# Batch 0 of a spectral filter ahead of an MLP: both filter products from one spectrum, the inverse tables built earlier, and matmuls on ones between the stages

## The chip, the cores and the metric

One core of a Trainium2 chip (trn2). The metric is the device time of one execution in microseconds (us), the median over runs. The kernel before takes 773.71 us (9 runs, 773.45 to 774.46).

## What is computed

The reference has two layers that follow each other. The first filters along the sequence in the frequency domain, the second is an MLP with an exact GELU. Cut to what matters:

```python
# x: (8, 3008, 256); filt_r, filt_i: (1505, 256); w_in: (256, 2048); w_out: (2048, 256)
X = np.fft.rfft(x, axis=1)
Y = X * (filt_r + 1j * filt_i)[None, :, :]
y = np.fft.irfft(Y, n=3008, axis=1).reshape(8 * 3008, 256)
h = y @ w_in
out = (0.5 * h * (1.0 + erf(h / np.sqrt(2)))) @ w_out
```

All arrays are float32 in DRAM. On the chip the operands are bf16 and the sums float32.

## The kernel before

**The transform.** 3008 = 47 x 64. A transform of that length is made as matmuls with small tables: a stage over 47 points (table `T1`, stage 1), a twiddle and a stage over 64 points (`T2`, stage 2), the product with the filter, the inverse over 64 points (`T3`, stage 3) and the inverse over 47 points (`T4`, stage 4). With real input 24 values of the first frequency index (`K1 = 24`) are enough, and they are worked on in 12 pairs p. The tables are not loaded: they are computed at the start. DVE makes angles (`table_1`, `table_2_angle`), ACT takes their sine, and the matrix with real and imaginary parts exchanged comes from a matmul with a signed permutation (`table_2_swap`, L194). `T3` is `T2` transposed on PE (`table_3`, L230).

**Batches 1 to 7.** Their four stages (`s1`, `s2`, `s3`, `s4`) are small and are spread between the matmuls of the MLP of the batch before, at slots that are written out by hand (`put`). A slot is one `mm2` step (4 matmuls with `w_out`, L488) and one `mm1` step (2 matmuls with `w_in`, L461, and a GELU on ACT, L464). Between `s1` and `s2`, and between `s3` and `s4`, the data go through DRAM (`R1`, `R2`) to be re-ordered. `r1` and `r2` read them back. For batch 1 the slots are a list of their own: first slots of `s1`, `s2`, `s4`, their spacing, and the slots of `r1` and `r2`.

**Batch 0.** Nothing can hide it: the MLP has no input before it is through. It runs in a form of its own which stays on the chip, with the channels on partitions where the other batches have the sequence:

- `c1` (L361), 16 steps u: stage 1 of a group of 4 columns and one half of the channels. Steps u = 0 to 3 need the first two of eight transfers of x, steps 4 to 7 the next two, and so on. ACT or DVE empties each result into `at_sb`.
- `c1t` (L371), 6 steps: 8 transposes on PE, emptied into `b_sb`.
- `c2` (L383, L388), 12 steps p: stage 2. The product with the filter needs (real, imaginary) times the filter's real part, and (-imaginary, real) times its imaginary part. Before, `T2` holds three columns (-imaginary part, real, imaginary), PE makes both forms of the spectrum with 4 matmuls, and one DVE multiplication over 128 x 1024 (L388) makes both products. The last pair is done in two halves (L392).
- `c3` (L405): stage 3, both products are summed in PSUM against the same `T3`. ACT empties it into `vt_sb`.
- `c3t`, `c4` (L424, L438): transposes and stage 4, into `y_sb`, which `mm1` reads.

The filter arrives in partitions 0 to 63 of `F` (`load_filters`, L91) and is needed in partitions 64 to 127 as well. Before, `dup_filters` (L96) copies it, for the pairs p = 0, 1 on DVE and for the other ten on POOL, one copy for each pair.

**What sets the order.** The program is under a manual schedule: every engine runs its instructions in the order in which the Python code issues them, and an instruction that waits holds up all that stand behind it on its engine. The only choice left is that of PSUM buffers. The order of the prelude is written out in the kernel's main function: table work is put between the steps of `c1` and `c2`. All loads of x, the filter and the MLP weights are issued by POOL, so they stand in one line with POOL's copies. `warm_up(n)` issues n matmuls of 512 columns on a tile of ones, whose results nobody reads.

Of the kernel before, what the change touches and what calls it, by code (L numbers as in the profile page):

```python
# [21 lines left out]
TCH = 512  # L22

# [5 lines left out]
class _Mix:  # L29
    def __init__(self, ctx, tc, x, filt_r, filt_i, w_in, w_out, out):  # L30
# [23 lines left out]
        self.T2 = c.tile([128, K1, 3, NB], BF16, name="T2")  # L54
# [19 lines left out]
    def load_x(self, b, lo=0, hi=4, hs=(0, 1)):  # L74
        nc = self.nc
        if lo == 0 and 0 in hs:
            self.st[b, "x"] = self.px.tile([128 if b else 2 * NA, HB, 256], BF16, tag="x", name="x_sb")
        xt, o = self.st[b, "x"], 64 if b else NA
        xv = self.x[b].rearrange("(n1 h c w) d -> h c n1 w d", h=2, c=4, w=8)
        for c in range(lo, hi):  # L80
            for h in hs:
                nc.gpsimd.dma_start(out=xt[h * o:h * o + NA, c * 8:c * 8 + 8, :], in_=xv[h, c])  # L82
# [14 lines left out]

    def gate(self, t):

        g = self.po.tile([1, 1], BF16, tag="gate", name="gate")  # L100
        self.nc.gpsimd.tensor_copy(out=g, in_=t)  # L101

    def load_next(self, b, p, c, h):

        self.gate(self.st[b, "p", p][0:1, 0:1])
        self.load_x(b + 1, c, c + 1, (h,))
# [17 lines left out]
    def table_1(self, g):  # L124
# [3 lines left out]
        k48 = self.iota(g, "k48", [128, 2, K1], [[0, 2], [1, K1]])  # L128
        off = g.tile([128, 2, K1], FP32, name="off")
        nc.gpsimd.memset(off[:, 0, :], 0.25)  # L130
        nc.gpsimd.memset(off[:, 1, :], 0.5)
# [7 lines left out]
        nc.vector.scalar_tensor_tensor(out=w, in0=k48, scalar=n1, in1=off, op0=ALU.mult, op1=ALU.add)  # L139
# [6 lines left out]
    def table_2(self, g):  # L146
# [8 lines left out]
        self.n2, ri = col("n2"), col("ri")  # L155
        v.tensor_copy(out=self.n2, in_=m_i)
        v.tensor_copy(out=ri, in_=ri_i)
        ts(out=self.n2, in0=self.n2, scalar1=1.0 / self.S, scalar2=None, op0=ALU.mult)
        ts(out=ri, in0=ri, scalar1=-0.25, scalar2=0.25, op0=ALU.mult, op1=ALU.add)
        self.jn = g.tile([128, NB], FP32, name="jn")  # L160
        ts(out=self.jn, in0=self.jj, scalar1=self.n2, scalar2=ri, op0=ALU.mult, op1=ALU.add)
        self.n12, self.sg, self.to = col("n12"), col("sg"), col("to")
        ts(out=self.n12, in0=self.n2, scalar1=float(K1 // 2), scalar2=None, op0=ALU.mult)

        ts(out=self.sg, in0=ri, scalar1=8.0, scalar2=-1.0, op0=ALU.mult, op1=ALU.add)
        v.tensor_tensor(out=self.to, in0=self.p, in1=self.sg, op=ALU.add)

    def unit_matrices(self, g, cols):
        ts = self.nc.vector.tensor_scalar
        self.eye, self.swap = (g.tile([128, 128], BF16, name=n) for n in ("eye", "swap"))  # L170
        ts(out=self.eye, in0=cols, scalar1=self.p, scalar2=None, op0=ALU.is_equal)
        ts(out=self.swap, in0=cols, scalar1=self.to, scalar2=self.sg, op0=ALU.is_equal, op1=ALU.mult)

    def table_2_angle(self, h):

        v, k = self.nc.vector, K1 // 2
        w, r = self.gen[:, h], self.gen[:, 2]
        if h == 0:
            v.scalar_tensor_tensor(out=w, in0=self.kk.unsqueeze(2).to_broadcast([128, k, NB]), scalar=self.n2,
                                   in1=self.jn.unsqueeze(1).to_broadcast([128, k, NB]), op0=ALU.mult, op1=ALU.add)  # L180
        else:
            v.tensor_scalar(out=w, in0=self.gen[:, 0], scalar1=self.n12, scalar2=None, op0=ALU.add)
        v.tensor_scalar(out=r, in0=w, scalar1=RND, scalar2=-RND, op0=ALU.add, op1=ALU.add)
        v.tensor_tensor(out=w, in0=w, in1=r, op=ALU.subtract)

    def table_2_sin(self, h):
        self.nc.scalar.activation(out=self.T2[:, 12 * h:12 * h + 12, 1, :], in_=self.gen[:, h], func=AF.Sin,
                                  scale=2.0 * PI)

    def table_2_swap(self, h):  # L190
        t2 = self.T2[:, 12 * h:12 * h + 12]
        for i in range(2):
            ps = self.bank("ps_sw", "n")
            self.nc.tensor.matmul(ps[:, 0:384], lhsT=self.swap, rhs=t2[:, :, 1, 32 * i:32 * i + 32],  # L194
                                  start=True, stop=True)
            self._evac(t2[:, :, 2, 32 * i:32 * i + 32], ps[:, 0:384].rearrange("p (k j) -> p k j", k=12),
                       "act", 1.0 - 2.0 * i)
            if h == 1:
                self._evac(t2[:, :, 0, 32 * i:32 * i + 32], ps[:, 0:384].rearrange("p (k j) -> p k j", k=12),
                           "act", 2.0 * i - 1.0)  # L200

    def table_2_minus(self):
        t2 = self.T2[:, 0:12]
        self.nc.vector.tensor_scalar(out=t2[:, :, 0, :], in0=t2[:, :, 2, :], scalar1=-1.0, scalar2=None, op0=ALU.mult)

    def weights_4(self, g):

        nc, v = self.nc, self.nc.vector
        ts = v.tensor_scalar
        col = lambda name: g.tile([128, 1], FP32, name=name)  # L210
        q, c = col("q"), col("c48")
        ts(out=c, in0=self.p, scalar1=48.0, scalar2=None, op0=ALU.is_ge)
        v.scalar_tensor_tensor(out=q, in0=c, scalar=-48.0, in1=self.p, op0=ALU.mult, op1=ALU.add)
        self.wt = col("wt")
        ts(out=self.wt, in0=q, scalar1=2.0, scalar2=1.0, op0=ALU.is_ge, op1=ALU.add)
        self.wtc = col("wtc")
# [10 lines left out]
    def table_3(self, q, eng):  # L227
        ps = self.bank("ps_t3", "n", BF16)
        for i in range(8):
            self.nc.tensor.transpose(ps[:, 128 * i:128 * i + 128],  # L230
                                     self.T2[:, 8 * q + i, 1:3].rearrange("p a b -> p (a b)"), self.eye)

        self._evac(self.T3[:, 8 * q:8 * q + 8], ps.rearrange("p (k n r) -> p k r n", k=8, r=2), eng)

    def warm_up(self, n):

        ps = self.bank("ps_warm", "w")
        for i in range(n):
            self.nc.tensor.matmul(ps[:, i % 2], lhsT=self.ones[:, 0:128], rhs=self.ones, start=True, stop=True)
# [50 lines left out]
    def s2(self, b, p):  # L290
        nc = self.nc
        ps = self.bank("ps_s2")
        for i in range(2):
            k = 2 * p + i
            nc.tensor.matmul(ps[:, 256 * i:256 * i + 256], lhsT=self.T2[:, k, 1:3].rearrange("p a b -> p (a b)"),  # L295
# [70 lines left out]
    def c1t(self, q, eng):  # L366
# [6 lines left out]
        self._evac(b[:, 0:4, :].rearrange("p a b -> p (a b)"), ps, eng)  # L373

    def c2(self, p):
# [4 lines left out]
        for t, o in ((0, 1), (1, 0)):  # L380
            for i in range(2):
                k = 2 * p + i
                nc.tensor.matmul(ps[:, t, 256 * i:256 * i + 256],  # L383
                                 lhsT=self.T2[:, k, o:o + 2].rearrange("p a b -> p (a b)"),
                                 rhs=self.st[0, "b", k // 4][:, k % 4, :], start=True, stop=True)
        f = self.F[:, :, 2 * p:2 * p + 2, :]
        if p < 11:
            nc.vector.tensor_tensor(out=w, in0=ps, in1=f.rearrange("p t a b -> p t (a b)"), op=ALU.mult)  # L388
            return
        w, ps = (v.rearrange("p t (a b) -> p t a b", a=2) for v in (w, ps))  # L390
        for c in (slice(0, 128), slice(128, 256)):
            nc.vector.tensor_tensor(out=w[:, :, :, c], in0=ps[:, :, :, c], in1=f[:, :, :, c], op=ALU.mult)  # L392

    def c3(self, p, np=2):

        if p == 0:
            self.vt = self.pg.tile([128, 2, 97, 32], BF16, tag="g", name="vt_sb")
        ps = [self.bank("ps_c3", "n") for half in range(2)]
        for i in range(np):
            w = self.st[0, "p", p + i]  # L400
            for half in range(2):
                for k in range(2):
                    for t in range(2):
                        c, o = 128 * (2 * i + k), 256 * k + 128 * half
                        self.nc.tensor.matmul(ps[half][:, c:c + 128], lhsT=w[:, t, o:o + 128],  # L405
                                              rhs=self.T3[:, 2 * (p + i) + k].rearrange("p a b -> p (a b)"),
                                              start=t == 0, stop=t == 1)
# [5 lines left out]
    def c3t(self, u):  # L413

        if u == 0:

            self.nc.gpsimd.memset(self.vt[:, :, 96, :], 0.0)
# [89 lines left out]
def kernel(  # L507
# [16 lines left out]
    m.psum(wide, w=(2, 2), n=(4, 1))  # L524
    act = "act"
    m.p = m.iota(g, "p", [128, 1], [[0, 1]], cm=1)
    m.load_x(0, 0, 1, (0,))
    m.pi = m.iota(g, "pi", [128, 1], [[0, 1]], cm=1, dt=I32)
    m.load_x(0, 0, 1, (1,))
# [4 lines left out]
    m.weights_4(g)  # L534
# [3 lines left out]
    m.kk = m.iota(g, "kk", [128, K1 // 2], [[1, K1 // 2]])  # L538
    m.jj = g.tile([128, NB], FP32, name="jj")
    for sgn, lo in ((1, 0), (-1, 32)):  # L540
        nc.gpsimd.iota(m.jj[:, lo:lo + 32], pattern=[[sgn * NA, 32]], base=min(0, sgn * NA),
                       channel_multiplier=0, allow_small_or_imprecise_dtypes=True)
    cols = m.iota(g, "cols", [128, 128], [[1, 128]])
    m.load_x(0, 1, 4)
    m.gen = m.py.tile([128, 3, K1 // 2, NB], FP32, tag="y", name="gen")
    m.table_2(g)
    m.table_2_angle(0)
    m.unit_matrices(g, cols)
    m.table_2_angle(1)
    for k, n in ((0, 4), (4, 4), (8, 8), (16, 8)):  # L550
        m.load_filters(k, n)
    m.dup_filters(nc.gpsimd, 4, 4)
    m.load_w_in()
    m.dup_filters(nc.gpsimd, 8, 8)


    warm = g.tile([128, 1], FP32, name="warm")
    for u in range(16):
        m.c1(u // 2, u % 2, act if u < 4 or u % 2 else False)
        if u == 3:  # L560
            m.warm_up(3)
            m.table_2_sin(0)
        if u == 7:
            m.table_2_swap(0)
            m.table_2_minus()
            m.warm_up(3)
            m.table_2_sin(1)
        if u == 11:
            m.warm_up(2)

    nc.scalar.activation(out=warm, in_=m.p, func=AF.Gelu)
# [113 lines left out]
```

## Time and profile before

| | us |
|---|---|
| median of 9 runs | 773.71 |
| the profiled execution, its own time | 773.71 |
| its span in the trace | 771.9 |

The 1.8 us between the last two lie around the span. Cutting the span at the points where the work changes gives, for busy times in us:

| stretch of the span | PE | DVE | ACT | POOL | what runs there |
|---|---|---|---|---|---|
| 0 to 5.8 | 4.34 | 3.33 | 1.84 | 4.77 | `warm_up`, `T1`, first transfers of x |
| 5.8 to 14.0 | 6.83 | 8.05 | 6.63 | 5.68 | `c1`, first half of the tables |
| 14.0 to 31.4 | 16.28 | 15.45 | 16.36 | 17.19 | `c1t`, `c2`, `c3`, `T3`, filter copies |
| 31.4 to 39.9 | 7.11 | 6.73 | 6.03 | 4.11 | `c3t`, `c4` |
| 39.9 to 50.3 | 10.14 | 9.06 | 7.46 | 0.00 | `mm1` of the first tile, `s1` of batch 1 |
| 50.3 to 771.9 | 713.08 | 354.54 | 529.00 | 32.79 | MLP, batches 1 to 7 between |

Busy times count an engine's overlapping instructions once. PE's ends are modelled, so a busy PE is not PE at its peak. The granted TensorE clock is 1.00 in every stretch. In the lists of the trace a row has its start, the time from the first start to the last end of the instructions merged in it, engine, line, operation, tiles and count. What stands in brackets is the engine's idle time before it and what ended it.

### The profile page before, as it was taken

The numbers are of one execution on the slowest core, as the hardware profiler recorded it, in microseconds if no ns is written. First come the engines' busy times: TensorE is split into PE (matmuls) and PEld (weight loads), VectorE is DVE, ScalarE is ACT, GpSimd is POOL, SyncE is SP. The second block draws the span as 40 slices with busy tenths as digits, with TensorE's granted clock in tenths as the row PEclk, the third lists the DMA queues.
The fourth block names the chain that finished last, engine by engine and source line by source line (L and its number), as shares of the span: only waits on it lengthen the run. The fifth ranks groups of instructions, "written<-read, shape, count | busy, mean of one in ns | idle before, by whom it ended". The sixth has DMA issues, their size and how long they took to land.

```text
span 771.9 us, 14958 instructions
## 1 busy us (share of the span) xinstructions
PE 757.8 (98%) x5965; PEld 528.4 (68%) x6066; DVE 397.1 (51%) x722; ACT 567.3 (73%) x981; POOL 64.5 (8%) x160
## 2 busy tenths in 40 slices
PE   8999999999999999999999999999999999999998
PEld 5847675676776766667677767666776776766666
DVE  8856755464555645457463664637646366411011
ACT  6879955897568975699656996579865798666663
POOL 8801100020000200011000110001100000000000
PEclk9999999999999999999999999999999999999999
DMA  9894745466154661636516464354553422410111
GB/s 144 144 192 115 151 114 126 131 126 157 49 140 109 136 161 41 191 77 127 139 53 181 85 133 123 80 153 98 121 137 82 138 83 69 123 42 28 42 42 55
DMA packets 87398, 85.66 MB, mean 111 GB/s; under 512 B 6752, under 2 KB 77536, under 8 KB 87328
## 3 DMA queue, kind: packets, MB, share of 16 engines
q1 hardware_dynamic: 78816, 68.70, 31.1%
q0 software_dynamic: 8512, 16.00, 14.1%
q8 instruction: 47, 0.77, 0.4%
q14 instruction: 23, 0.19, 0.1%
HBM read 54.00 MB, written 46.66 MB: 130 GB/s over the span
## 4 chain that ended last, share of the span: by engine, by line
PE 92%; POOL 3%; DMA 2%; issue 1%; ACT 1%; DVE 0%; POOLq 0%; SPq 0%
PE ps_o L488 43%; PE ps_h L461 39%; PE ps_s L320 3%; PE ps_s L345 3%; PE ps_s L295 2%; PE ps_s L272 2%; DMA x_sb<-in_x_dram 2%; POOL F L96 1%; POOL x_sb L82 1%; POOL F L91 1%; DMA d_sb<-R 0%; PE ps_e L478 0%; ACT g_sb L464 0%; ACT p L301 0%; ACT p L302 0%
## 5 line engine op out<-in xcount | busy, mean ns | idle before, releaser
L464 ACT ACTIVATE g_sb<-ps_h 128x512 bf16<-128x512 f32 x752 | 437.9, 597 | 183.4 <-PE ps_h L461 155.4
L488 PE MATMUL ps_o<-w_out_sb,g_sb 128*128 128x256 bf16 x2992 | 447.8, 273 | 2.0
L461 PE MATMUL ps_h<-y_sb,w_in_sb 128*128 128x512 bf16 (+3 forms) x1500 | 424.8, 366 | 0.8 <-DMA x_sb<-in_x_dram 0.7
L488 PEld LDWEIGHTS <-g_sb 128*128 128x128 bf16 x2992 | 283.6, 98 | 134.5 <-issue 9.9
L461 PEld LDWEIGHTS <-w_in_sb 128*128 128x128 bf16 x1600 | 154.6, 98 | 23.9 <-issue 1.1
L494 DVE COPY ost<-ps_o 128x512 f32<-128x512 f32 x93 | 63.8, 686 | 143.5 <-PE ps_o L488 143.5
L303 DVE TENSOR_TENSOR p<-ps_s,F 128x512 bf16<-128x512 f32 x84 | 58.1, 691 | 105.9 <-ACT p L302 89.4
L249 DVE TENSOR_SCALAR y_sb<-ps_s 128x376 bf16<-128x376 f32 x112 | 60.9, 548 | 80.9 <-PE ps_s L345 80.9
L247 DVE CAST a_sb<-ps_s 128x512 bf16<-128x512 f32 x112 | 69.3, 682 | 27.7 <-PE ps_s L272 27.7
L247 DVE CAST v_sb<-ps_s 128x512 bf16<-128x512 f32 x84 | 57.3, 684 | 3.0 <-PE ps_s L320 3.0
L301 ACT ACTIVATE p<-ps_s 64x512 bf16<-64x512 f32 x84 | 49.8, 593 | 2.0
L302 ACT CAST p<-ps_s 64x512 bf16<-64x512 f32 x84 | 48.5, 577 | 1.0
L345 PEld LDWEIGHTS <-d_sb 96*128 96x128 bf16 x448 | 30.8, 97 | 25.8 <-DMA d_sb<-R 0.7
L101 POOL COPY gate<-p 1x1 bf16<-1x1 bf16 x48 | 8.5, 176 | 470.8 <-DVE p L305 470.8
L345 PE MATMUL ps_s<-T,d_sb 96*128 96x94 bf16 x448 | 36.4, 205 | 1.5 <-DMA d_sb<-R 0.4
L305 DVE TENSOR_TENSOR p<-p 128x512 bf16<-128x512 bf16 x84 | 35.7, 425 | 2.9
L304 DVE TENSOR_TENSOR p<-p,F 128x512 bf16<-128x512 bf16 x84 | 34.8, 415 | 0.0
L320 PE MATMUL ps_s<-p,T 128*128 128x256 bf16 x168 | 32.1, 273 | 2.2 <-DVE p L305 0.2
L82 POOL DMA_DIRECT2D x_sb<-in_x_dram x64 | 32.5, 510 | 13.1 <-issue 12.6
L295 PE MATMUL ps_s<-b_sb,T 128*128 128x256 bf16 x168 | 32.1, 273 | 0.0
L320 PEld LDWEIGHTS <-T 128*128 128x128 bf16 x168 | 16.3, 98 | 20.1 <-DVE p L305 0.5
L295 PEld LDWEIGHTS <-T 128*128 128x128 bf16 x168 | 16.4, 98 | 13.4
(103 smaller groups left out, 189.5 us busy)
## 6 DMA issues: line engine op xcount, KB each, us to landing
out_dram<-ost SPq DMA_DIRECT2D x93, 256.0 KB, 2.4
x_sb<-in_x_dram POOLq DMA_DIRECT2D x64, 188.0 KB, 3.6
R<-a_sb SPq DMA_DIRECT2D x112, 96.0 KB, 2.1
b_sb<-R SPq DMA_DIRECT2D x28, 384.0 KB, 4.1
R<-v_sb SPq DMA_DIRECT2D x42, 256.0 KB, 3.3
d_sb<-R SPq DMA_DIRECT2D x56, 192.0 KB, 4.6
w_in_sb<-in_moe_w_in_dram POOLq DMA_DIRECT2D x2, 512.0 KB, 8.0
w_out_sb<-in_moe_w_out_dram POOLq DMA_DIRECT2D x2, 512.0 KB, 11.5
```

The costliest lines, as they stand in the source:

```text
L247: self.nc.vector.tensor_copy(out=out, in_=in_)
L249: self.nc.vector.tensor_scalar(out=out, in0=in_, scalar1=scale, scalar2=None, op0=ALU.mult)
L295: nc.tensor.matmul(ps[:, 256 * i:256 * i + 256], lhsT=self.T2[:, k, 1:3].rearrange("p a b -> p (a b)"), rhs=self.st[b, "b", k // 6][:, k % ...
L301: nc.scalar.activation(out=p2[0:64], in_=ps[64:128], func=AF.Copy, scale=-1.0)
L302: nc.scalar.copy(out=p2[64:128], in_=ps[0:64])
L303: nc.vector.tensor_tensor(out=p1, in0=ps, in1=f(0), op=ALU.mult)
L320: nc.tensor.matmul(ps[:, 256 * i:256 * i + 256], lhsT=self.T3[:, k].rearrange("p a b -> p (a b)"), rhs=w[:, 256 * i:256 * i + 256], start= ...
L345: nc.tensor.matmul(ps[:, 94 * i:94 * i + 94], lhsT=d[:, (grp % 2) * 4 + i, 128 * half:128 * half + 128], rhs=t4, start=True, stop=True)
L461: nc.tensor.matmul(ps[:, o:o + n], lhsT=self.w_in_sb[:, dc, jc * 128:jc * 128 + 128], rhs=self.ring[:, dc, off:off + n], start=(dc == 0), ...
L464: nc.scalar.activation(out=self.st["g", t][:, jc, :], in_=ps, func=AF.Gelu)
L488: nc.tensor.matmul(ps[:, tile_i % 2, :], lhsT=g[:, jc, tile_i * 128:tile_i * 128 + 128], rhs=self.w_out_sb[:, jc, :], start=(jc == 0), sto ...
L494: nc.vector.tensor_copy(out=ost, in_=ps)
```

## The change

- **One spectrum.** `T2` loses its third column. `c2` makes 2 matmuls into one PSUM bank instead of 4 into two, and the DVE multiplication reads this bank twice (a broadcast operand of the same 128 x 1024 elements). The factor i goes into a second inverse table `T3i`: `c3` multiplies the product with the filter's imaginary part by `T3i`. `T3i` is `T3` with its two columns exchanged and a sign for each partition; it is made by two DVE instructions for k = 0 to 7 and two for 8 to 15 (`table_3_turn`), and by two ACT instructions from PSUM for 16 to 23.
- **Angles by shifts.** The angle in turns is kept between 64 and 128, so that a left shift of its bits by 15 leaves the fraction as a signed 32-bit integer; ACT reads that and scales it by 2 pi / 2^32. This takes the place of two rounding passes per half.
- **Table order.** The first sine stands ahead of `c1` u = 0 on ACT instead of behind u = 3. The swap of the first half, and the transposes of `T3` for k = 0 to 7, stand on PE between `c1` u = 3 and u = 4 (before: the swap behind u = 7, the transposes among the `c2` steps). The second sine and its swap stand between u = 7 and u = 8 (before: the sine there, the swap behind `c2` p = 1). The second third of `T3` stands ahead of `c1t`. `T4c`'s matmul moves from q = 4 to u = 11.
- **Filter.** Three parts of 8 instead of 4, 4, 8, 8. Its second copy is made by DVE for p = 0, 1, by a transfer from SBUF to SBUF on the SP queue for p = 2, 3 and p = 8 to 11, and by POOL for p = 4 to 7.
- **Issue order on POOL.** The first two transfers of x stand ahead of the index tile `p`; `w_in`'s loads move behind the copies, directly ahead of x of batch 1. Some small constants move from DVE to POOL or back.
- **The rest.** 42 matmuls on ones instead of 20. PSUM is cut otherwise (w, m, n = 2, 1, 5 banks; then v, t = 4, 4 instead of 5, 3). The GELU table is loaded behind the last `c3` instead of behind `c1`. `c1t` 0 is emptied in two halves. For batch 1, `s1`, `r1` and `s2` each start one slot earlier.

The core of the diff:

```diff
-        self.T2 = c.tile([128, K1, 3, NB], BF16, name="T2")
+        self.T2 = c.tile([128, K1, 2, NB], BF16, name="T2")
...
+    def dup_filters_dma(self, k0, k):
+        self.nc.sync.dma_start(out=self.F[64:128, :, k0:k0 + k, :], in_=self.F[0:64, :, k0:k0 + k, :])
...
+            v.scalar_tensor_tensor(out=w[:, 0:6], in0=self.kk.unsqueeze(2).to_broadcast([128, 6, NB]), scalar=self.n2,
+                                   in1=jn.unsqueeze(1).to_broadcast([128, 6, NB]), op0=ALU.mult, op1=ALU.add)
+            ts(out=w[:, 6:12], in0=w[:, 0:6], scalar1=n6, scalar2=None, op0=ALU.add)
+        else:
+            ts(out=w[:, 12:24], in0=w[:, 0:12], scalar1=self.n12, scalar2=None, op0=ALU.add)
+        k = slice(12 * h, 12 * h + 12)
+        ts(out=self.gen[:, 1, k].bitcast(I32), in0=w[:, k].bitcast(I32), scalar1=15, scalar2=None,
+           op0=ALU.logical_shift_left)
...
-        v.tensor_scalar(out=r, in0=w, scalar1=RND, scalar2=-RND, op0=ALU.add, op1=ALU.add)
-        v.tensor_tensor(out=w, in0=w, in1=r, op=ALU.subtract)
...
+    def table_3_turn(self, q):
+        k = slice(8 * q, 8 * q + 8)
+        for r in range(2):
+            self.nc.vector.tensor_scalar(out=self.T3i[:, k, r, :], in0=self.T3[:, k, 1 - r, :],
+                                         scalar1=self.turn[r], scalar2=None, op0=ALU.mult)
...
-        for t, o in ((0, 1), (1, 0)):
-            for i in range(2):
-                nc.tensor.matmul(ps[:, t, 256 * i:256 * i + 256],
-                                 lhsT=self.T2[:, k, o:o + 2].rearrange("p a b -> p (a b)"),
+        for i in range(2):
+            nc.tensor.matmul(ps[:, 256 * i:256 * i + 256], lhsT=self.T2[:, k].rearrange("p a b -> p (a b)"),
...
-            nc.vector.tensor_tensor(out=w, in0=ps, in1=f.rearrange("p t a b -> p t (a b)"), op=ALU.mult)
+            nc.vector.tensor_tensor(out=w, in0=ps.unsqueeze(1).to_broadcast([128, 2, 512]),
+                                    in1=f.rearrange("p t a b -> p t (a b)"), op=ALU.mult)
...
+                        t3 = (self.T3i if t else self.T3)[:, 2 * (p + i) + k]
...
+    for k in range(0, K1, 8):
+        m.load_filters(k, 8)
+    m.dup_filters_dma(4, 4)
+    m.dup_filters_dma(16, 8)
+    m.table_2_sin(0)
     for u in range(16):
-        m.c1(u // 2, u % 2, act if u < 4 or u % 2 else False)
+        m.c1(u // 2, u % 2, False if u in (1, 3, 5, 7, 8, 9, 10, 12, 14) else act)
         if u == 3:
             m.warm_up(3)
-            m.table_2_sin(0)
+            m.table_2_swap(0)
+            m.table_2_angle(g, 1)
+            m.table_3(0)
         if u == 7:
-            m.table_2_swap(0)
-            m.table_2_minus()
             m.warm_up(3)
             m.table_2_sin(1)
+            m.table_2_swap(1)
+            m.warm_up(2)
+        if u == 10:
+            m.table_3_turn(0)
         if u == 11:
+            m.table_4(m.T4c, m.T1q, m.wtc)
             m.warm_up(2)
+    m.table_3(1)
+    m.warm_up(1)
+    m.c1t(0, False)
+    m.table_3_turn(1)
+    m.dup_filters(nc.vector, 0, 4)
+    m.c1t(1, act)
+    m.dup_filters(nc.gpsimd, 8, 8)
...
-            s1, n1, r1, s2, n2, r2, s4, n4 = 1, 4, 16, 26, 2.8, 61, 68, 0.72
+            s1, n1, r1, s2, n2, r2, s4, n4 = 0, 4, 15, 25, 2.8, 61, 68, 0.72
```

## The prediction, made before the changed kernel had run

> **What bounds the kernel now.** I read the page's busy shares first, then the table by stage, then the waits of PE in the MLP, and last the timeline of the first 45 us. The page, busy time and share of the span:
>
> ```profile
> PE 757.8 (98%) x5965; PEld 528.4 (68%) x6066; DVE 397.1 (51%) x722; ACT 567.3 (73%) x981; POOL 64.5 (8%) x160
> ```
>
> PE is the bound on average, but the change touches PE's main work nowhere: the stretch from 50.3 us keeps its matmuls. So the answer lies ahead of 39.9 us and in a few waits behind it. By stage, the columns are length, then busy time of PE, PEld, DVE, ACT, POOL, granted clock, DMA share, GB/s:
>
> ```profile
> 5.80:14.00 8.20, 6.83 (x76) 4.50 (x76) 8.05 (x16) 6.63 (x14) 5.68 (x12) 1.00 1.05 182
> 14.00:31.40 17.40, 16.28 (x215) 14.28 (x215) 15.45 (x16) 16.36 (x29) 17.19 (x27) 1.00 0.85 132
> ```
>
> In the second of these every engine looks full, but PE's busy time holds matmuls that start behind each other with waits in their modelled ends. The groups of DVE from 14 to 32 us (shape, count, busy, mean ns, idle before and its releaser) tell what sets the pace:
>
> ```profile
> L388 DVE TENSOR_TENSOR p<-ps_c,F 128x1024 bf16<-128x1024 f32 x11 | 12.8, 1216 | 1.2 <-POOL F L96 1.0
> L392 DVE TENSOR_TENSOR p<-ps_c,F 128x512 bf16<-128x512 f32 x2 | 1.3, 679 | 0.0
> ```
>
> And the timeline of the prelude (start, duration, engine, line, what, idle before):
>
> ```profile
> 1.46 4.45 PE L239 MATMUL ps_warm<-ones 128*128 128x512 bf16 x10 [1.46 <-DVE h L133]
> ...
> 8.39 0.84 ACT L187 ACTIVATE T<-gen 128x768 bf16<-128x768 f32 x1 [0.46 <-DVE gen L184]
> ...
> 9.67 0.70 PE L194 MATMUL ps_sw<-T,swap 128*128 128x384 bf16 x2 [0.63 <-ACT at_sb L245]
> ...
> 10.85 1.39 PE L361 MATMUL ps_c<-T1c,x_sb 94*128 94x96 bf16 x16
> ...
> 14.04 1.08 PE L371 MATMUL ps_c1t<-eye,at_sb 128*128 128x128 bf16 x16
> ...
> 16.23 4.83 DVE L388 TENSOR_TENSOR p<-ps_c,F 128x1024 bf16<-128x1024 f32 x4
> ...
> 21.80 6.88 DVE L388 TENSOR_TENSOR p<-ps_c,F 128x1024 bf16<-128x1024 f32 x6 [0.74 <-POOL F L96]
> ...
> 28.98 1.23 DVE L388 TENSOR_TENSOR p<-ps_c,F 128x1024 bf16<-128x1024 f32 x1 [0.31 <-POOL F L96]
> ```
>
> So three steps follow each other: until 16.2 us PE and ACT make tables and `c1` in turn; from 16.23 to 31.40 DVE's multiplications are the chain; then 8.5 us of `c3t` and `c4`. Only the middle step waits for POOL's copies.
>
> **What the change does to each step.**
>
> Start to `c1`. Two x transfers (0.69 and 0.51 us on POOL, L82) go ahead of `p`, so DVE's chain starts some 1.6 us later and loses its constants; by those rows `T1c` is ready about 4.9 instead of 4.6 us. Not on the path: `c1` u = 0 starts at 5.78 behind ten spare matmuls, 0.43 us each, which stay. Cost 0; a delay of the table by over 0.9 us would show.
>
> The angle. Now L179 1.01, L183 0.56, L184 0.96 for 768 columns. After: L179 and L182 (0.61) at half size, about 0.55 and 0.36, then one shift of 768. The trace has no integer shift; its bounds are L183's 0.56 and L184's 0.96, and I take 0.56, as it too reads one tensor. From L204's 0.35 for 768 bf16 columns it could also be 0.2 less. With `jn` (0.31) the angle is ready at about 6.8, 1.6 us earlier than now, and the first sine (0.84) ends at 7.7 instead of 9.23.
>
> The order on PE. This is the main term. Behind `c1` u = 3 stand the swap (2 x 0.16) and 8 transposes of `T3` (L371's 8 take 0.61), all ahead of u = 4. ACT runs: sine to 7.7, two evacuations of `c1`, two of the swap (pitch 0.38 to 0.49), to 9.2. Transposes to 9.9, and u = 4 starts there instead of 8.20. ACT's copy of `T3` (0.91 pitch) to 10.8, `c1` u = 4 and 6 to 11.6, second sine to 12.45. Its swap holds PE until 12.95, two spare matmuls 0.4, so u = 8 starts at 13.3 instead of 10.85. From there DVE has six `c1` evacuations (L247, 0.465 pitch) and now two `table_3_turn` ones. Nearest row: L204, 768 bf16 columns, 0.35; 512 columns then 0.28 each. Upper bound 0.68 (L247 on 512 columns). That ends at 16.5, `c1t` 0 starts at 16.6 (now 14.04), its evacuation in two halves ends at 18.0, another turn 0.44, two copies for p = 0, 1 (0.42 each): the first multiplication at 19.0 instead of 16.23. **+2.8 us.**
>
> [...] If PE let `c1` pass, the 2.8 would be some 0.3.
>
> The multiplications. Eleven at 1.13 pitch (the four from 16.23 and the six from 21.80), then 0.60 and 0.68: 13.7 us, against 31.40 - 16.23 = 15.17 now. The difference of 1.47 is the waits for POOL (0.12, 0.74, 0.31) and lost overlap. The element count is unchanged, so reading one bank twice is priced at nothing. From above it is bounded by two L392 halves, 1.36; from below by two of L304 (512 columns, both operands bf16 in SBUF, 0.415), 0.83, which would take up to 4 us off. The row it is nearest to is L388 itself, with the same types and the same PSUM source, so I keep 1.216 and leave the floor in the share outside the range. Dropping 24 matmuls of 256 columns saves PE 24 x 0.11 = 2.6 us beside DVE, so 0 on the path; 22 more spare matmuls at 0.21 give 4.7 back, also in gaps. What is late next: the product p = 8 waits on PE for the last `T3` transposes, 16 `c3` matmuls and a spare one, about 0.4. **-1.1 us.** So the middle ends at about 33.1 instead of 31.40.
>
> Filter copies. POOL then copies four pairs instead of ten, 1.04 us each (L96). The parts of the filter land at 13.7, 15.3, 19.6 and 22.3 now; the third is the one POOL waits for, so it is done by 23.5, when p = 4 is due (19.0 + 4 x 1.13). The trace has no SBUF to SBUF transfer. The 256 KB for p = 2, 3 should land near 18.5 and is due at 21.3 (19.0 + 2 x 1.13). The 512 KB for p = 8 to 11 can be issued when the last filter part landed, about 22.5, and is due at 28.5. Nearest rows, median us to landing: 192 KB 4.6, 384 KB 4.1, 512 KB 8.0 (L111's `w_in`, in a full queue). That gives 26.6 to 30.5: 0 to +2.0, and I take 0, as the SP queue holds nothing else there, and add half a us to the upper end for the shared engines. SP's queue behind it holds only `R1` writes, first at 42.87.
>
> `w_in` is issued behind POOL's copies at 24.4 instead of 19.6; with 8.0 it lands by 32 to 34, x of batch 1 by 40. `mm1` needs `w_in` at about 41.8: hidden, with 8 us of cover.
>
> The tail. Four `v` banks instead of five: +0.2. The GELU table load leaves ACT's `c1` and falls behind the last `c3`, where ACT now idles 2.29 us ahead of its first `y_sb` row: 0, and 1.28 us (the load's row, L571) if that gap were gone.
>
> Batch 1. PE's waits behind 40 us are few:
>
> ```profile
> PE ps_h L461 <- DMA x_sb<-in_x_dram: 0.7, 1, 0.7
> PE ps_s L345 <- DMA d_sb<-R: 0.4, 1, 0.4
> ```
>
> The first stands for `y_sb`'s last evacuations, which end just ahead of it; `s1` now stands in front of it but its PSUM banks come free with the same evacuations, so 0. The second, at 101.26, goes, as the last `R2` write is a slot earlier: **-0.4 us**. `r1`'s slack of 1.6 us (landed 57.40, used 59.02) shrinks by 0.4, still covered.
>
> **Sum.** +2.8 - 1.1 + 0.2 - 0.4 = +1.5 to +1.6. The profiled execution's own time equals the median, so 773.7 + 1.6 = **775.3**.
>
> [...] The trace's row: the first ten run at 0.43 pitch, later ones at about 0.21, and PE has no idle of 0.8 us behind them. [...]
>
> **Rivals.** What a measurement can tell is 0.2%, 1.55 us: faster is below 772.16, slower above 775.26.
>
> A, the forecast: 774.5 to 776.4, as the turns and waits vary by their bounds. It lies across the upper bound, half on each side. 0.52.
>
> B, faster: the table steps don't hold PE, because ACT gets through its steps in the gaps (shorter sine, evacuations on the other engine) and u = 8 still starts near 10.85. Then the first product is at 16.4, the middle ends at 30.5 (30.1 without the wait at p = 8), and -0.9 + 0.2 - 0.4 gives 772.6, or 772.2; with the lost overlap gone too, 772.0. For it: ACT is 6.63 of 8.20 us busy there, so it has some room, and the angle is 1.6 us earlier. Against: the chain sine, swap, copy, sine, swap is written in series on two engines. Each us by which u = 8 comes ahead of 13.3 takes one us off; the sign turns at 11.7. 0.22, of it 0.14 below 772.16.
>
> C, slower: the late copy of the filter rows holds p = 8 by up to 2.5 us on top of A: 775.5 to 777.8. For it: the engines move 132 GB/s in this stage and are 85% busy. 0.17.
>
> D, slower: turns at 0.68 each and a shift at 0.96, or PE cold in a gap so that `c1` runs at double pitch: +0.4 to +1.5 on A, up to 776.8. 0.09.
>
> That the change doesn't do what it says would be C's cousin: waits for POOL's copies leave and the same product waits for the SP transfer.
>
> Range 772.0 to 777.8. Faster 0.14, same 0.08 + 0.25 = 0.33, slower 0.27 + 0.17 + 0.09 = 0.53.
>
> **What to look for after.** `c1`'s third block of 16 matmuls at 13.3 (B: 11); first multiplication at 19.0, last end at 33.1; no wait of a multiplication for POOL or for a transfer into `F` (C: one at p = 8); `mm1` first at about 42; the `d_sb` wait gone; `c1t` at 0.06 us a matmul (D: 0.12). If the first multiplication starts ahead of 17.5, or a pitch under 1.0 shows there, the forecast is wrong.

## The result and the profile after

The changed kernel takes 776.85 us (median of 9 runs, 776.67 to 779.66) against 773.81 (29 runs of the kernel before, 773.33 to 774.79): a ratio of 1.0043 (95% interval 1.0034 to 1.0051), 3.0 us slower. The profiled execution took 777.39 with a span of 775.6, 3.7 us over the span before. One run of experiment 7 (801.19 us, granted clock 0.942) was in a slow state, so it is left out of that run's median and its trace isn't read. The page's busy shares hardly move:

```profile
PE 758.1 (98%) x5960; PEld 527.3 (68%) x6064; DVE 397.6 (51%) x727; ACT 566.8 (73%) x977; POOL 59.5 (8%) x158
```

The table by stage, cut at the new stage bounds (same columns as before: length, busy time of PE, PEld, DVE, ACT, POOL, clock, DMA share, GB/s):

```profile
14.00:19.50 5.50, 4.61 (x62) 3.44 (x60) 4.73 (x13) 3.89 (x7) 2.75 (x5) 1.00 1.10 157
19.50:35.58 16.08, 12.73 (x158) 10.39 (x160) 13.91 (x13) 11.26 (x18) 9.33 (x17) 1.00 0.83 158
35.58:44.21 8.63, 7.75 (x136) 6.82 (x135) 6.73 (x11) 7.70 (x19) 2.32 (x3) 1.00 1.16 203
44.21:775.60 731.39, 723.09 (x5533) 501.67 (x5633) 363.78 (x656) 536.41 (x921) 32.76 (x96) 1.00 0.43 109
```

The stage of the products is 16.08 us long and DVE is busy for 13.91 of it. The groups of DVE there name the missing 2 us, and it is a transfer and not POOL:

```profile
L411 DVE TENSOR_TENSOR p<-ps_c,F 128x1024 bf16<-128x1024 f32 x11 | 12.7, 1216 | 2.2 <-DMA F<-F 2.0
L416 DVE TENSOR_TENSOR p<-ps_c,F 128x512 bf16<-128x512 f32 x2 | 1.3, 679 | 0.0
```

The timeline of the prelude, the rows that answer to those of before:

```profile
6.92 0.84 ACT L209 ACTIVATE T<-gen 128x768 bf16<-128x768 int32 x1 [2.23 <-DVE gen L183]
...
7.81 0.70 PE L216 MATMUL ps_sw<-T,swap 128*128 128x384 bf16 x2 [0.39 <-DVE eye L205]
...
9.34 0.62 PE L242 MATMUL ps_t<-eye,T 128*128 128x128 bf16 x8 [0.82 <-ACT T L268]
...
9.79 0.84 PE L384 MATMUL ps_c<-T1c,x_sb 94*128 94x96 bf16 x16
...
12.56 0.48 PE L216 MATMUL ps_sw<-T,swap 128*128 128x384 bf16 x2 [1.27 <-ACT T L209]
...
13.31 0.85 PE L384 MATMUL ps_c<-T1c,x_sb 94*128 94x96 bf16 x16
...
16.75 1.07 PE L394 MATMUL ps_c1t<-eye,at_sb 128*128 128x128 bf16 x16 [0.68 <-DVE at_sb L270]
...
19.50 2.36 DVE L411 TENSOR_TENSOR p<-ps_c,F 128x1024 bf16<-128x1024 f32 x2
...
23.88 10.51 DVE L411 TENSOR_TENSOR p<-ps_c,F 128x1024 bf16<-128x1024 f32 x9 [2.02 <-DMA F<-F]
```

The first product starts 3.27 us later than before, the third waits 2.02 us for the SBUF transfer of its filter rows, and from there nine run at a pitch of 1.13, with one longer step, 1.36, at p = 8. In the MLP the wait for `d_sb` is gone from PE's list.

The ledger of the span, before to after: first product +3.27 (16.23 to 19.50), products +0.91 (15.17 to 16.08), tail +0.11 (8.52 to 8.63), all behind it -0.59 (731.98 to 731.39). Sum +3.70, the difference of the two spans.

### The profile page after: what moved, and what is told of

Same layout as the page of the kernel before. It is cut to its first block, busy times and chain, and to the rows that moved or that the text cites. A ratio compares the mean times of both kernels' runs of the same rounds, so it can differ in the third digit from the quotient of the medians.

```text
span 775.6 us, 14954 instructions
## 1 busy us (share of the span) xinstructions
PE 758.1 (98%) x5960; PEld 527.3 (68%) x6064; DVE 397.6 (51%) x727; ACT 566.8 (73%) x977; POOL 59.5 (8%) x158
## 4 chain that ended last, share of the span: by engine, by line
PE 94%; DMA 2%; POOL 1%; issue 1%; ACT 1%; DVE 1%; POOLq 0%; DVEq 0%; SPq 0%; ACTq 0%
PE ps_o L508 43%; PE ps_h L481 39%; PE ps_s L343 3%; PE ps_s L368 3%; PE ps_s L318 2%; PE ps_s L295 2%; DMA F<-F 1%; ACT y_sb L268 1%; DMA F<-in_filt_i_dram 1%; POOL x_sb L83 1%; PE ps_c L429 0%; DVE p L411 0%; PE ps_c L407 0%; PE ps_e L498 0%; POOL F L92 0%
## 5 line engine op out<-in xcount | busy, mean ns | idle before, releaser
L481 PEld LDWEIGHTS <-w_in_sb 128*128 128x128 bf16 x1600 | 154.6, 98 | 23.6 <-issue 1.6
```

Source lines behind the costliest of these rows:

```text
L481: nc.tensor.matmul(ps[:, o:o + n], lhsT=self.w_in_sb[:, dc, jc * 128:jc * 128 + 128], rhs=self.ring[:, dc, off:off + n], start=(dc == 0), ...
```

## The experiments

Every time is a median beside runs of the kernel before in the same session and on the same chip (773.76 to 773.96). The changed kernel's 776.85 is from another session, with 773.81 beside it.

**1. The transfer, replaced by POOL.**

```diff
-    m.dup_filters_dma(4, 4)
+    m.dup_filters(nc.gpsimd, 4, 4)
```

> The changed kernel with the second copy of the filter rows for p = 2, 3 made by POOL instead of by the SP transfer. Theory (the 2.02 us wait of the third multiplication is the price of that transfer alone): POOL is free from 18.0, its two copies are done by 20.1, due at 21.9, so the wait goes whole: 776.85 - 2.0 = 774.8, multiplications 0 to 7 at 1.13 pitch. Rival (the transfer only hides the next late thing): p = 8 is then due at about 28.7 and the other SP transfer lands at about 28.6, or POOL's copies for p = 4 to 7 come late; half or more is given back, 775.8 or above.

Measured: 779.52, ratio 1.0065 (1.0048 to 1.0082), 2.7 us slower than the changed kernel. Neither theory had the reason. The wait for the transfer is gone, but the first product starts at 22.56 instead of 19.50. The timeline of DVE and POOL shows why:

```profile
18.15 0.98 DVE L255 TENSOR_SCALAR T3i<-T,turn_r 128x512 bf16<-128x512 bf16 x1
19.05 1.12 DVE L255 TENSOR_SCALAR T3i<-T,turn_i 128x512 bf16<-128x512 bf16 x1
20.21 2.32 DVE L97 COPY F<-F 64x1024 bf16<-64x1024 bf16 x2
22.56 3.49 DVE L411 TENSOR_TENSOR p<-ps_c,F 128x1024 bf16<-128x1024 f32 x3
```

```profile
17.95 6.46 POOL L97 COPY F<-F 64x1024 bf16<-64x1024 bf16 x6
```

DVE's four instructions from SBUF to SBUF take 0.98, 1.12 and twice 1.2 us beside POOL's copies of 1.1 us each; in the changed kernel, where POOL is idle at that time, the same ones take 0.34, 0.34 and 0.42. DVE's products, which read PSUM, keep 1217 ns each with POOL copying beside them. PE then has nothing for 4.41 us and its next matmuls run at about half speed: 8 transposes took 1.06 us instead of 0.61, the first matmuls of `c3` (from 26.38) have a pitch of 0.105 us and the later ones 0.055, and the granted clock of the stretch from 22 to 26 us was 0.68. Of the six runs five had a mean clock of 0.996 to 0.998 and took 778.05 to 781.08; the one at 1.00 took 775.62, 1.2 under the changed kernel. So what this edit costs differs from run to run; whether DVE was held up in the fast one no trace shows.

**2. The transfer, replaced by DVE.**

```diff
-    m.dup_filters_dma(4, 4)
-    m.dup_filters(nc.vector, 0, 4)
+    m.dup_filters(nc.vector, 0, 8)
```

> The changed kernel with the second copy of the filter rows for p = 2, 3 made by DVE, behind its copies for p = 0, 1, in place of the SP transfer; POOL stays as it is. Theory (the SP transfer costs 2.02 us, and POOL's copies beside DVE's copies were what made the POOL version slow): two more copies at 0.42 put the first multiplication at 20.3, no wait at p = 2: 776.85 + 0.8 - 2.0 = 775.6, and DVE's copies and turns keep 0.42 and 0.34. Rival (the wait only moves to the next filter rows, POOL's for p = 4 or the other SP transfer): 776.5 or above. Rival 2 (DVE's copies are slow for another reason than POOL's): they take 1.1 again, and the time is 778 or above.

Measured: 776.10, ratio 1.0029 (1.0018 to 1.0041), 0.75 under the changed kernel where 1.25 was expected. The first product starts at 20.21, eight run without a gap, and 0.30 comes back at p = 8, where DVE waits for PE. DVE's group rows decide between the two causes of experiment 1, the same instructions without POOL beside them:

```profile
L97 DVE COPY F<-F 64x1024 bf16<-64x1024 bf16 x4 | 1.4, 416 | 0.0
L255 DVE TENSOR_SCALAR T3i<-T,turn_i 128x512 bf16<-128x512 bf16 x1 | 0.3, 346 | 0.0
L255 DVE TENSOR_SCALAR T3i<-T,turn_r 128x512 bf16<-128x512 bf16 x1 | 0.3, 345 | 0.0
```

So POOL's copies were the cause, and rival 2 falls.

**3. The first third of the filter earlier.**

```diff
     m.unit_matrices(g, cols)
+    m.load_filters(0, 8)
     m.turn_signs(g)
...
-    for k in range(0, K1, 8):
+    for k in range(8, K1, 8):
```

> The changed kernel with the first third of the filter (k = 0 to 7) loaded by POOL ahead of its small constants and T1q instead of behind them, 3.7 us earlier; the SP transfer for p = 2, 3 stays. Theory (that transfer is late because it is issued late, at 17.26): the part lands at about 15.3 as in the kernel before, the transfer starts 1.9 us earlier and with the same 6.5 us lands at 21.9, when p = 2 is due: 774.8 to 775.1. Rival (it is late because it shares the engines with the loads queued beside it, so an earlier start is only a slower transfer): it lands at 23 or later and 776 or above is left.

Measured: 776.06, ratio 1.0028 (1.0017 to 1.0038): 0.8 us of the 2.0 come back, nearer to the rival. The transfer is issued at 15.72 instead of 17.26, 1.54 earlier, and lands at 22.60 instead of 23.78, only 1.18 earlier: it takes 6.9 us instead of 6.5. In both kernels it lands as the last filter loads do (22.85 and 24.20). The DMA view of the changed kernel has the comparison in itself:

```profile
F<-F SPq DMA_DIRECT2D x1, 512.0 KB, 4.4
...
F<-F SPq DMA_DIRECT2D x1, 256.0 KB, 6.5
```

Twice the bytes, issued when the filter had landed, took 4.4 us. The 256 KB beside the queued loads took 6.5. From 17.26 to 23.78 the DMA engines moved 159 GB/s in all, and the 256 KB are about 40 of it; from 24.28 to 28.65 they moved 131, and the 512 KB are about 120 of it. Late issue is shown by this run; shared engines are the reading of these two rows, as no run has the 256 KB alone.

**4. The table steps moved out of PE's way, alone.** Two spare matmuls behind the second swap go with them, and ACT instead of DVE makes the turned `T3` for k = 8 to 15.

```diff
         if u == 3:
...
-            m.table_3(0)
         if u == 7:
             m.warm_up(3)
             m.table_2_sin(1)
-            m.table_2_swap(1)
-            m.warm_up(2)
-        if u == 10:
-            m.table_3_turn(0)
+            m.table_3(0)
         if u == 11:
+            m.table_2_swap(1)
...
-    m.table_3(1)
+    m.table_3_turn(0)
     m.warm_up(1)
     m.c1t(0, False)
-    m.table_3_turn(1)
...
-        if q == 3:
-            m.table_3(2, turn=True)
+        if q in (2, 3):
+            m.table_3(q - 1, turn=True)
```

> The changed kernel with the table steps alone moved out of the way on PE, as in the run named order; the filter loads and both SP transfers stay as in the changed kernel. Theory (the order on PE and the late transfer are two limits in parallel, and the later one counts): the first multiplication comes at about 17.1, but p = 2 still waits until the transfer lands at about 23.8, so the wait grows to 4.4 us, and the time stays within 0.5 of 776.85, or goes above it when PE, idle for 4 us, runs slow after that. Rival (the two costs add up): 776.85 - 2.4 = 774.4.

Measured: 777.45, ratio 1.0052 (1.0038 to 1.0066). DVE's products:

```profile
17.37 2.36 DVE L411 TENSOR_TENSOR p<-ps_c,F 128x1024 bf16<-128x1024 f32 x2
23.01 7.01 DVE L411 TENSOR_TENSOR p<-ps_c,F 128x1024 bf16<-128x1024 f32 x6 [3.28 <-DMA F<-F]
```

The first product comes at 17.37, 2.1 us earlier, although DVE's copies ahead of it now wait 0.75 for the first third of the filter, and nothing is won: the wait for the transfer (landed 22.92) is 3.28 us. The order on PE and the transfer lie side by side up to p = 2, and the later one counts. Two of the five runs were 1.5 us above the other three at a clock of 0.998; PE has a gap of 3.02 us in that wait.

**5. Both limits taken away: edits 1, 3 and 4 together.**

> The two edits above together (copy for p = 2, 3 on POOL, first third of the filter early), and the table steps put out of the way on PE: T3 for k = 0 to 7 behind c1 u = 7, the second swap behind u = 11, T3 for k = 8 to 15 among the products with its turned form made by ACT. Theory (in-order PE held by table steps costs the prelude 2.5 to 3 us): c1 u = 8 starts at about 11 instead of 13.3 and the first multiplication at 16.5 to 17.4 instead of 19.5; the products then run into the SP transfer for p = 8 to 11, due at about 26 and landing at 26.7 to 28: 772.5 to 774. Rival (ACT's work is the limit and PE only shows its waits): c1 u = 8 stays behind 12.5, the first multiplication behind 18.7, 774.3 or above.

Measured: 773.41 (11 runs), ratio 0.9997 (0.9988 to 1.0005): level with the kernel before, 3.4 us under the changed one. The third block of `c1` and the products:

```profile
11.43 0.84 PE L384 MATMUL ps_c<-T1c,x_sb 94*128 94x96 bf16 x16 [1.05 <-DMA x_sb<-in_x_dram]
```

```profile
17.07 6.88 DVE L411 TENSOR_TENSOR p<-ps_c,F 128x1024 bf16<-128x1024 f32 x6
24.14 2.35 DVE L411 TENSOR_TENSOR p<-ps_c,F 128x1024 bf16<-128x1024 f32 x2 [0.20 <-POOL T1s L279]
26.96 3.48 DVE L411 TENSOR_TENSOR p<-ps_c,F 128x1024 bf16<-128x1024 f32 x3 [0.46 <-PE ps_c L407]
```

`c1` now waits for x, as it should. POOL's copies of p = 2, 3 start at 16.86, when DVE's are nearly through (0.79 for two). The SP transfer for p = 8 to 11, issued at 21.90 with the filter landed, is down at 26.57, just in time. The first product is still 0.84 later than in the kernel before (17.07 against 16.23), and the stage of the products 0.61 shorter (14.56 against 15.17), so even here the prelude wins nothing.

**6. The slots of batch 1 alone, on the kernel before.**

```diff
-            s1, n1, r1, s2, n2, r2, s4, n4 = 1, 4, 16, 26, 2.8, 61, 68, 0.72
+            s1, n1, r1, s2, n2, r2, s4, n4 = 0, 4, 15, 25, 2.8, 61, 68, 0.72
```

> The kernel before with the slots of batch 1 alone one earlier (s1, r1, s2). Theory: the wait of 0.44 us for d_sb goes and nothing new comes: -0.4, 773.4. Rival: the time stays at 773.8, because s1 ahead of the first mm1 or r1's shorter slack gives it back.

Measured: 773.56 (11 runs), ratio 0.9994 (0.9986 to 1.0003). The wait for `d_sb` is off PE's list and the time 0.3 lower, as forecast in sign and size, but the interval takes in no change.

**7. The spare matmuls.** Three runs: the changed kernel without any but the first ten, the changed kernel without those behind `c1t` 0, and the kernel before without any but the first ten (every other `m.warm_up(...)` line taken out).

> The changed kernel without its spare matmuls behind the first ten (32 fewer). Theory (they buy nothing, as PE has no gap of 3 us): the same time or up to 0.4 less, 776.4 to 776.9, transposes of c1t at 0.06 a piece. Rival (gaps of 2 us, in the waits at 11, 20 and 24 us, are enough for PE to fall to half speed, as behind the gap of 4.41 us in the run with POOL's copies): c1t at twice that, and 1 to 3 us more.

> The changed kernel with its spare matmuls up to c1t 0 kept, and those behind it (among the products) left out. Theory (in the run without any, the clock fell at about 10 us, in the gaps that the tables leave on PE, so only the early ones count): clock 1.00, the wait of 0.30 at p = 8 gone, 776.5. Rival (the gap of 2 us where p = 2 waits for the transfer is enough without the spare matmuls around it): clock 0.998 or lower, 777.5 to 779.

> The kernel before without its ten spare matmuls behind the first ten. Theory (its PE gaps in the prelude stay under 1.5 us, and what fills them is real work): 773.4 to 774.2, clock 1.00. Rival (PE falls to half speed at about 10 us as in the changed kernel without them): clock 0.993, 775 or above.

Measured: 777.99 with ratio 1.0053 (1.0039 to 1.0067); 776.97 with 1.0045 (1.0032 to 1.0057); 775.65 with 1.0021 (1.0012 to 1.0030). The rivals' times hold for the first and the third, at clocks of 0.991 to 0.993 and 0.993 to 0.996; where the clock fell in the first no trace shows. In the kernel before without them, PE's timeline:

```profile
8.13 0.84 PE L361 MATMUL ps_c<-T1c,x_sb 94*128 94x96 bf16 x16 [0.87 <-DMA x_sb<-in_x_dram]
9.67 0.70 PE L194 MATMUL ps_sw<-T,swap 128*128 128x384 bf16 x2 [0.70 <-ACT at_sb L245]
11.20 1.44 PE L361 MATMUL ps_c<-T1c,x_sb 94*128 94x96 bf16 x16 [0.83 <-DMA x_sb<-in_x_dram]
13.08 1.44 PE L361 MATMUL ps_c<-T1c,x_sb 94*128 94x96 bf16 x16 [0.44 <-DMA x_sb<-in_x_dram]
14.85 2.03 PE L371 MATMUL ps_c1t<-eye,at_sb 128*128 128x128 bf16 x16 [0.33 <-DVE at_sb L247]
```

and its table in steps of 4 us, the clock third from the end:

```profile
6.00:10.00 4.00, 2.42 (x33) 1.95 (x31) 3.86 (x8) 3.24 (x7) 2.79 (x6) 1.00 1.03 171
10.00:14.00 4.00, 2.68 (x30) 2.20 (x30) 3.47 (x7) 2.79 (x7) 2.06 (x5) 0.59 1.10 181
14.00:18.00 4.00, 3.67 (x31) 2.98 (x29) 2.43 (x6) 3.46 (x6) 4.00 (x8) 0.56 1.01 130
```

The last two blocks of 16 `c1` matmuls take 1.44 us each (1.39 and 0.98 in the kernel before), and the 16 transposes of `c1t` 2.03 instead of 1.08, after a stretch whose longest gap is 0.87 us. With the spare matmuls PE is busy for 3.02 of the 4 us from 6 to 10 (kernel before), without them for 2.42, and the clock falls. The share of 4 us alone doesn't decide it: the second run has 2.41 in the same stretch and keeps 1.00. The second of the three runs lies between: three of its five runs are at 776.6 to 777.0 with clock 1.00, two at 778.2 to 778.4 with 0.996 and 0.998. There the fall comes among the products, behind a stretch with 1.96 of 4 us busy (18 to 22), at 0.53.

**8. Two tries at something better.** The first builds on experiment 5: filter parts of 4, 4, 8, 8, DVE's copies for p = 0, 1 ahead of `c1t` 0, the turned `T3` on ACT, POOL's copies up to p = 9, no spare matmuls among the products.

> A version that the runs point to. From the run named order (773.41): filter in parts of 4, 4, 8, 8 with the first early; DVE copies p = 0, 1 ahead of c1t 0, in its idle time; POOL copies p = 2 to 9 only when DVE's copies are through, the SP transfer only p = 10, 11; ACT instead of DVE turns T3 for k = 0 to 7; no spare matmuls from c1t 1 on; PSUM of the tail as in the kernel before (5, 3). Theory: the first multiplication at 16.3 instead of 17.1, no wait at p = 8 (0.46), 0.1 in the tail: 773.4 - 1.3 = 772.1, 1.6 to 1.8 under the kernel before. Rival (POOL's copies or the loads of w_in and x of batch 1, now 2 us later, hold the products or mm1): 773 or above.

Measured: 778.86, ratio 1.0057 (1.0043 to 1.0071): the rival. The first product starts at 16.94 (16.3 in the forecast), two products wait for POOL's copies (0.82 and 0.25), and the last ends at 31.93, 0.3 behind experiment 5. POOL is through with its copies at 27.0 instead of 23.6, `w_in`, x and `w_out` are issued behind them, and `w_out` lands at 52.36 instead of 46.70 (both against experiment 5). `R1`'s writes stand in that traffic, 6.1 to 7.3 us to landing instead of 2.3 to 4.3, and `s1` of batch 1 waits for their buffer. DVE's timeline, then PE's waits behind 40 us:

```profile
52.22 2.48 DVE L269 CAST a_sb<-ps_s 128x512 bf16<-128x512 f32 x4 [3.21 <-DMA R<-a_sb]
```

```profile
PE ps_h L480 <- DVE a_sb L269: 2.7, 1, 2.7
```

The granted clock fell to 0.81 there. Its two fastest runs, at clock 1.00, are at 776.7 and 776.9.

The second takes experiment 5 and only leaves out the spare matmuls behind `c1t` 0:

> The run named order without spare matmuls from c1t 1 on. Theory: the waits of 0.20 and 0.46 us of the products for PE shrink by about 0.4, and PE has work enough there to keep its clock: 773.0. Rival (the spare matmuls among the products hold the clock): clock below 0.999 and 774 or above.

Measured: 773.51, ratio 0.9994 (0.9985 to 1.0003), clock 1.00 in all 11 runs: no measurable difference to experiment 5. The wait of 0.20 went, that of 0.46 stayed (0.49): so the spare matmuls, which are gone there, aren't its cause; PE has the transposes and `c3` ahead of it.

**9. The kernel before with its own waits for POOL removed.** Slots as in experiment 6, and

```diff
-    m.load_w_in()
     m.dup_filters(nc.gpsimd, 8, 8)
+    m.load_w_in()
```

> A version that the runs point to: the kernel before, with the slots of batch 1 one earlier (as in the run named slots) and w_in's two loads issued behind POOL's copies for p = 4 to 7 instead of ahead of them. Theory (POOL's copy for p = 4 starts 1.1 us late because of these issues, and the later waits follow from it): the waits of 0.74 and 0.31 us for POOL go, w_in lands at 30 to 32, due at 40: 773.6 - 1.0 = 772.5. Rival (the copies are late because the filter lands late, and x of batch 1, issued behind, comes later): 773.3 or above.

Measured: 773.35 (11 runs), ratio 0.9991 (0.9982 to 1.0000), the lowest median of the study, about 0.6 under the kernel before, at the edge of what the interval can tell. The waits for POOL's filter copies are gone from the profile; 0.3 at p = 10 is put down to POOL though its tables were done, so its releaser is another, not settled. The profiled execution shows how thin the cover is: x of batch 0 came late, PE was idle for 1.67 us ahead of `c1` u = 4, the clock fell to 0.70 from 10 to 14 us, and the first product started at 17.41 instead of 16.23.

## Why the prediction was right, and where it was not

The forecast was 775.3, slower, with a range of 772.0 to 777.8; 776.85 lies inside, on the side of slower. It lies above the forecast's own band (A, 774.5 to 776.4) and in that of rival C (775.5 to 777.8), so the sum was too low and the range held through C. Step by step:

- **Angle and first sine: right.** The shift took 0.56, the halves 0.61 and 0.42, the sine ended at 7.76 (7.7 forecast).
- **PE in series: right, and shown by experiments 4 and 5.** `c1` u = 4 at 9.79 (9.9 forecast), u = 8 at 13.31 (13.3), `c1t` 0 at 16.75 (16.6). Rival B falls. The kernel before has such a wait too: the swap's first weights are loaded at 8.87, its matmul starts at 9.67 behind 0.63 us of idle PE, and `c1` u = 8, which stands behind it, at 10.85. With the steps moved, u = 8 starts at 11.05 to 11.43 and waits for x.
- **First product: +3.27, not +2.8.** The prediction's own last terms, 18.0 + 0.44 + 2 x 0.42, add up to 19.3 and not to the 19.0 that it wrote. The turns took 0.34 to 0.42 each, not 0.28, and the last pair 0.60 instead of 0.44; `c1t` started only 0.15 later, since DVE had five results of `c1` to empty there and not six: two errors that offset each other.
- **The products: +0.91 instead of -1.1, the term that failed.** Without the transfer's wait the stage is 16.08 - 2.02 = 14.06 us, and 14.1 was forecast (33.1 - 19.0), so the price of the multiplications was right and reading one bank twice cost nothing (1216 ns both times). The 0.4 at p = 8 was 0.23 here and 0.30 in experiment 2. What was wrong is the sentence "The 256 KB for p = 2, 3 should land near 18.5". It landed at 23.78. The prediction gives no working for 18.5. The filter's first third landed at 17.16 and not at 15.3 as in the kernel before, since its loads were issued from 10.10 instead of 6.38, behind 3.6 us of small constants on POOL, whose issue order the prediction hadn't followed past the x loads; and the transfer took 6.5 us beside the other loads where the nearest rows had 4.1 to 4.6.
- **Rival C had the right mechanism at the wrong place.** It put the late copy at p = 8 to 11, priced at up to 2.5; that transfer was in time, and the other one cost 2.0.
- **Batch 1 and tail: right.** -0.59 behind the prelude (-0.4 forecast for `d_sb`; where the other 0.19 comes from no run shows), +0.11 in the tail (+0.2).
- **The spare matmuls "buy nothing", the theory of experiment 7: wrong.** The ten in the kernel before are worth 1.7 us (775.65 without them, 773.96 with), and those in the changed kernel keep its clock too (0.991 to 0.993 without them). I had gone by PE's longest gap, and the runs don't bear that out (last section). How many of the 22 added ones are needed was not tried; without those behind `c1t` 0 three of five runs show no difference and two take 1.4 us more.

By terms, forecast and span: +2.8 and +3.27; -1.1 and +0.91; +0.2 and +0.11; -0.4 and -0.59. The sum of the forecast missed by 2.0 in one term and by little in all others.

## What to carry to other kernels

The copy that was moved to another queue had two prices here: when it could be issued (17.26), and, in the reading of experiment 3, what it shared the engines with (6.5 us for its 256 KB beside the filter's loads, 4.4 for 512 KB behind them). Both followed from the issue order of the loads before it, so walk that queue instruction by instruction. Two limits that lie side by side don't add up: taking away the transfer alone (experiment 2) brought 0.75, the order on PE alone (experiment 4) nothing, both together (experiment 5, with the first third of the filter loaded earlier too) 3.4. In a prelude where PE waits, look at the granted clock of a run without its spare matmuls (0.993 to 0.996 in the kernel before, 0.999 to 1.00 with them) before calling them idle work.

## What the runs showed of the hardware that I had not expected

- **DVE's instructions from SBUF to SBUF took longer beside POOL's copies.** In experiment 1 DVE's bf16 instructions with both sides in SBUF took 984, 1125 and twice 1198 ns beside POOL's copies, about the length of one POOL copy, and in experiment 2 the same ones took 345, 346 and 416 ns without them. POOL's copies took 1120 ns in the mean instead of 1033, while DVE's products from PSUM kept 1217 ns. That is the price in this case; the cause of it no trace shows.
- **A fall of PE's clock lasted about 3.4 us, or twice that.** While it is down, the matmuls of `c3` run at a pitch of 0.105 to 0.107 us instead of 0.055 (experiment 1 from 26.38, the second run of experiment 7 from 22.56), about half speed. With half speed in it, the granted clock in steps of 4 us gives an estimate of the time below full speed: 3.4 us in experiment 1 (0.68 and 0.90 from 22 to 30), 3.4 in the first try of experiment 8 (0.81 and 0.76 from 50 to 58), 3.4 in experiment 9 (0.88 and 0.70 from 6 to 14), and 6.9 and 6.8 in the second and third run of experiment 7 (0.53 and 0.61 from 22 to 30; 0.59 and 0.56 from 10 to 18).
- **Neither the longest gap nor PE's busy time just before tells when it falls.** In the kernel before without spare matmuls the clock fell with no gap over 0.87 us. In the profiled run of experiment 4 it stayed at 1.00 through a gap of 3.02 us, from 21.28 to 24.30. The steps of 4 us also put the falls at about 23.4 us (experiment 1), 52.5 (experiment 8), 22.3 and 10.7 (experiment 7) and 9.0 (experiment 9). By PE's rows, PE was busy for about 0.0, 1.2, 1.4, 1.5 and 1.7 of the 3.4 us ahead of them; at the gap of experiment 4 it was busy for at most 0.4 of 3.4 us, and nothing fell. Two of that kernel's five runs, neither of them profiled, have a clock of 0.998, so the same program does both. What decides stays open.
